# Linear attention on one core: the outputs of paired heads stored head by head

## The chip, the cores and the metric

The kernel runs on 1 core of one Trainium2 chip. The metric is the device time of one execution in microseconds. Before the change it is 180.78 us, the median of 3 runs (179.79 to 180.81).

A core has five engines that run their own instruction streams: PE (TensorE, matmuls), DVE (VectorE), ACT (ScalarE), POOL (GpSimd) and SP (SyncE, here used to issue DMA transfers). They are ordered against each other by semaphores only. Data move between the chip's main memory (DRAM in the names below) and the on-chip SBUF, which has 128 partitions, by 16 DMA engines. A transfer names two lists of addresses, one for each side, as nested steps and counts.

## The reference, cut to what matters

```python
B, H, S, D = 1, 32, 2048, 128        # q, k, v: [B, H, S, D] bf16

def reference(q, k, v):
    phi_q = jnp.where(q > 0, q + 1, jnp.exp(q)) + 1e-6
    phi_k = jnp.where(k > 0, k + 1, jnp.exp(k)) + 1e-6
    kv = jnp.einsum("bhsd,bhse->bhde", phi_k, v)
    z = jnp.einsum("bhsd->bhd", phi_k)
    num = jnp.einsum("bhqd,bhde->bhqe", phi_q, kv)
    den = jnp.einsum("bhqd,bhd->bhq", phi_q, z)[..., None] + 1e-6
    return num / den
```

Each of the 32 heads has 2048 rows of 128 numbers in q, k, v and in the output, 512 KB each.

## The kernel before

**Work per head.** k and v of a head are loaded whole (512 KB, 128 partitions of 16 rows, 4 KB each). phi is made in two parts that are added in PSUM by matmuls: `em` = min(exp(x), 1) + EPS and `rk` = max(x, 0). The matmuls `kv{h}` (L430) build the 128 x 129 matrix of kv and z, `kvs{h}` (L397) copies it to SBUF. q is transposed on PE (`T`, L445) to PSUM, from which ACT and DVE make its two parts (L465 and L386, L392). The matmuls `n{h}.{i}` (L495 to L502) give numerators and denominators, `r` (L522) takes reciprocals and `f{h}.{i}` (L526, DVE) writes the quotients to the output buffer `o_sb[:, h % NO]`, with NO = 14 buffers of one head each. A store `st` then takes them to DRAM.

**Paired heads.** Heads 4 to 27 (`pair(h)`, L23) are handled in twos for q. One 1 MB load brings q of two heads as 128 partitions of 8 KB: 64 partitions for each head, 32 rows in each partition. After the transposes the columns of the two heads are sorted apart, in the order j, head, b, r. So in the output buffer of a paired head, partition 64 b + r holds rows 32 r + 16 b + j of that head, for j from 0 to 15. The first 64 partitions (b = 0) hold the even blocks of 16 rows (4 KB), the other 64 (b = 1) the odd blocks.

**The stores before.** Unpaired heads are stored from 128 partitions in one or more parts given by `st_parts` (L536). Head 2 goes in rows 0:51, 51:115 and 115:128 (`ROWS`), head 3 in two halves of its tiles, the first of them in rows 0:68 and 68:128 (`HALF`), head 31 in three parts of its tiles. A pair is stored by two transfers (L543), one for each half c of the partitions: 64 partitions, two heads, 4 KB. Each waits for every `f` of both heads.

**What sets the order.** The order of the instructions on each engine is written out by hand (`ORDER`, L108). SP issues all loads but one and all stores, one after another; an instruction that waits on SP holds up all that stand behind it. `add` registers an operation with what it depends on, `fill` and `used` add the waits for a buffer's earlier users, and `resolve` turns them into semaphore waits. After the last load (`ldq31.0`) SP has the stores st16, st24, st20, st23, st21, st18, st28, st19, st27, st22, st29, st26, st30 and the three of head 31. At the end SP waits for the semaphores of all output buffers (L562).

Of the kernel before, what the change touches and what calls it, by code (L numbers as in the profile page):

```python
# [14 lines left out]
NO, NE, NR, NV, NQ, NK = 14, 2, 2, 2, 4, 2  # L15
# [7 lines left out]
def pair(h):  # L23
    return QFIRST <= h < QLAST
# [36 lines left out]
def groups(h):  # L61
    if h == NH - 1:
        return ((0, 2, 3, 0), (6, 2, 3, 2), (12, 2, 2, 4))
    return ((0, 4, 3, 0), (12, 2, 2, 4))
# [6 lines left out]
def st_parts(h):  # L71
    tiles = ((0, 6), (6, 12), (12, 16)) if h == NH - 1 else WHOLE
    if h in HALF:
        tiles = HALVES
    return tuple((a, b, x, y) for i, (a, b) in enumerate(tiles)
                 for x, y in (HALF.get(h, ()) if i == 0 and h in HALF else ROWS.get(h, ((0, P),))))
# [5 lines left out]
def eps_dve(h, i):  # L82
    return i == 1 or h in EPD


def on(key, eng):
    return ON.get(key, eng)
# [90 lines left out]
def _ap(base: bass.AP, elem_offset: int, dims):  # L178
    return bass.AP(base.tensor, base.offset + elem_offset, [list(base.ap[0])] + [list(d) for d in dims])


class Program:
# [10 lines left out]
    def add(self, eng, key, fn, deps=(), dma=None, inc=True):  # L193
        assert key not in self.op, key
        self.op[key] = (eng, fn, tuple(deps), dma, inc)
# [71 lines left out]
def bass_standalone__linear_attn_elu__prompt_kernel(nc: bass.Bass, q: bass.AP, k: bass.AP, v: bass.AP, out: bass.AP):  # L267
    B, H, S, D = q.shape
    assert D == P and S == 16 * P and B * H == NH
    NT = S // P  # L270
# [5 lines left out]
    qf, kf, vf, of = (t.rearrange("b h s d -> (b h) s d") for t in (q, k, v, out))  # L276
    rows = lambda t, h: t[h].rearrange("(p j) d -> p j d", j=NT)

    with ExitStack() as es:
# [17 lines left out]
        o_sb = sb([P, NO, NT, D])  # L297
# [8 lines left out]
        add = pr.add  # L306
# [3 lines left out]
        def over(name, h, parts, t0, t1):  # L310
            return [f"{name}{h}.{i}" for i, (a, b) in enumerate(parts(h)) if a < t1 and t0 < b]

        def every(name, h, parts):
            return [f"{name}{h}.{i}" for i in range(len(parts(h)))]

        def fill(buf, n, heads, key):
            slots = [(buf, h % n) for h in heads]
            for s, h in zip(slots, heads):
                if users.get(s, (None, None, None))[0] != h:
                    users[s] = (h, users[s][2] if s in users else [], [])  # L320
            return [d for s in slots for d in users[s][1]]

        def used(buf, n, heads, key):
            for h in heads:
                u = users[buf, h % n]
                assert u[0] == h, (buf, h, u[0])
                u[2].append(key)

        def fs(h, banks):
            return [f"f{h}.{i}" for i, (t0, nb, n, b0) in enumerate(groups(h))  # L330
                    if set(banks) & set(range(b0, b0 + nb))]

        def both(h, p=pair):
            return (h - h % 2, h - h % 2 + 1) if p(h) else (h,)

        def first(h):
            return both(h)[0]

        def rqs(h, t0=0, t1=NT):
            return [d for x in both(h) for d in  # L340
                    ([f"rqa{x}"] if t0 < na(x) else []) + over("rqb", x, rqb_parts, t0, t1)]
# [57 lines left out]
        def head(h):  # L399
# [75 lines left out]
            if blk == len(two) - 1:  # L475
                for x in two:
                    out_of(x)

        def out_of(h):
            two, h0 = both(h), first(h)  # L480
            blk = h - h0

            def tile(buf, t):
                if len(two) == 1:
                    return buf[:, h % NQ, t]
                return buf[:, h0 % NQ:h0 % NQ + 2].rearrange("p h j d -> p (h j d)")[:, (2 * t + blk) * P:(2 * t + blk + 1) * P]

            for i, (t0, nb, m, b0) in enumerate(groups(h)):
                late = eps_dve(h, i)

                def g(e, t0=t0, nb=nb, m=m, b0=b0, late=late):
                    for b in range(nb):
                        o = 512 * (b0 + b)
                        if not late:
                            e.matmul(_ap(o_ps[:, :], o + D, [[NC, m]]), lhsT=ones[:], rhs=epsr[:, 0:m], start=True,  # L495
                                     stop=False, skip_group_check=True)
                        for c in range(m):
                            t = t0 + b * m + c
                            to = o_ps[:, o + NC * c:o + NC * (c + 1)]
                            e.matmul(to, lhsT=tile(emq_sb, t), rhs=kvs_sb[:, h % NK, 0:NC], start=late and c == 0,  # L500
                                     stop=False, skip_group_check=True)
                            ins = e.matmul(to, lhsT=tile(rq_sb, t), rhs=kvs_sb[:, h % NK, 0:NC], start=False, stop=True,  # L502
                                           skip_group_check=True)
                    return ins
                banks = range(b0, b0 + nb)
                t1 = t0 + nb * m
                key = f"n{h}.{i}"
                add("PE", key, g, [d for x in two for d in over("emq", x, q_parts, t0, t1)] + [f"kvs{h}", "ones", "eps1", "eps2"] + rqs(h, t0, t1)
                    + (fs(h - 1, banks) if h else []) + ([f"kvs{h + 1}"] if 5 in banks and h + 1 < NH else []))
                for buf, n in (("emq", NQ), ("rq", NQ)):  # L510
                    used(buf, n, two, key)
                used("kvs", NK, (h,), key)
                den = _ap(o_ps[:, :], 512 * b0 + D, [[512, nb], [NC, m]])
                rden = rden_sb[:, h % 2, t0:t1].rearrange("p (a b) -> p a b", b=m)
                done = [key]
                if 5 in banks and h + 2 < NH and GAP == 3:
                    done += every("kv", h + 2, kv_parts) if on(f"kvs{h + 2}", "DVE") == "DVE" else [f"kvs{h + 2}"]
                if late:
                    add("DVE", f"a{h}.{i}", lambda e, rden=rden, den=den: e.tensor_scalar(  # L519
                        rden, den, EPS, None, op0=ALU.add), done)  # L520
                    done, den = [f"a{h}.{i}"], rden
                add("DVE", f"r{h}.{i}", lambda e, rden=rden, den=den: e.reciprocal(rden, den), done)  # L522

                def g(e, t0=t0, t1=t1, nb=nb, m=m, b0=b0):
                    first = lambda t: t.offset
                    return e.tensor_tensor(  # L526
                        out=_ap(o_sb[:, :, :, :], first(o_sb[:, h % NO, t0, 0:1]) - first(o_sb[:, :, :, :]),
                                [[m * D, nb], [D, m], [1, D]]),
                        in0=_ap(o_ps[:, :], 512 * b0, [[512, nb], [NC, m], [1, D]]),
                        in1=_ap(rden_sb[:, :, :], first(rden_sb[:, h % 2, t0:t0 + 1]) - first(rden_sb[:, :, :]),  # L530
                                [[m, nb], [1, m], [0, D]]), op=ALU.mult)
                add("DVE", f"f{h}.{i}", g, [f"r{h}.{i}"] + fill("o", NO, (h,), f"f{h}.{i}"))
            if len(two) == 1:
                for i, (a, b, x, y) in enumerate(st_parts(h)):
                    key = f"st{h}.{i}"
                    add("SP", key, lambda e, a=a, b=b, x=x, y=y: e.dma_start(rows(of, h)[x:y, a:b], o_sb[x:y, h % NO, a:b]),  # L536
                        [f"f{h}.{j}" for j, (t0, nb, m, b0) in enumerate(groups(h)) if t0 < b and a < t0 + nb * m],
                        dma=f"o{h % NO}")
                    used("o", NO, (h,), key)
            elif blk:  # L540
                for c in range(2):
                    key = f"st{h0 + c}.0"
                    add("SP", key, lambda e, c=c: e.dma_start(  # L543
                        of[h0:h0 + 2].rearrange("h (r b j) d -> b r h (j d)", b=2, j=NT)[c],
                        o_sb[64 * c:64 * c + 64, h0 % NO:h0 % NO + 2].rearrange("p h j d -> p h (j d)")),
                        [d for x in two for d in every("f", x, groups)], dma=f"o{(h0 + c) % NO}")
                    used("o", NO, two, key)

        for h in range(NH):
            head(h)  # L550
# [40 lines left out]
```

## Time and profile before

| | |
|---|---|
| median of 3 runs | 180.78 us |
| the profiled execution's own time | 180.66 us |
| its span, first to last instruction | 179.4 us |
| PE busy | 155.6 us (87%) |
| DVE busy | 157.2 us (88%) |
| ACT busy | 146.8 us (82%) |
| POOL busy | 82.4 us (46%) |
| DRAM read / written | 50.33 MB / 16.78 MB |
| SP's issue of a paired store (L543), min/median/max | 0.60 / 1.85 / 2.67 us |
| paired store, issue to landing, min/median/max | 8.0 / 13.7 / 17.6 us |
| SP's waits for buffers and results at loads (L382 and L243) | 45 us |
| SP's waits for DVE at paired stores | 7.1 us |

How to read the profile: the page gives busy times by engine, then the span in 40 equal slices in which a digit is the busy share in tenths, then the DMA queues with their packets. A packet is one contiguous run of bytes moved by one DMA engine. The DMA row is the mean busy share of the 16 engines, and GB/s is what they moved together. "Windows" are the same sums for chosen stretches: start and end in us, length, then busy time and number of instructions of PE, PE's weight loads, DVE, ACT and POOL, then the granted PE clock, the DMA share and GB/s. Lines such as L543 are lines of the kernel.

### The profile page before, as it was taken

To read this page: it belongs to the slowest core of one execution; us is meant where nothing else is said; L and a number is where in the kernel's file an instruction comes from. 1 tells how busy PE (TensorE), PEld (TensorE's weight loads), DVE (VectorE), ACT (ScalarE), POOL (GpSimd) and SP (SyncE) were. 2 spreads that over 40 slices of the span, in tenths; PEclk is the share of its full clock that TensorE was granted. 3 is DMA by queue.
4 is the path that set the end of the run, shared out by engine and by line. 5 is a ranking of instruction groups with operands and counts; after the bars stand their busy time and mean duration, and the time that the engine had idled before them with its cause. 6 is when DMAs were issued, how large, how long until landed. Compare 5 with 4: busy or idle time off the path is not lost.

```text
span 179.4 us, 6127 instructions
## 1 busy us (share of the span) xinstructions
PE 155.6 (87%) x2709; PEld 150.2 (84%) x2709; DVE 157.2 (88%) x309; ACT 146.8 (82%) x99; POOL 82.4 (46%) x62
## 2 busy tenths in 40 slices
PE   6589997899999999999999999999995999994000
PEld 2279987899999999999999999999995999994000
DVE  0499999999999999999999999999989999999200
ACT  3879979799999999999999999999879897880000
POOL 1000512866675666666656666666566468100000
PEclk9999999999999999999999999999999999999755
DMA  6999999999999999999999999999999999999995
GB/s 234 408 422 410 412 408 420 407 407 420 405 418 400 420 407 407 371 388 410 418 422 417 408 407 396 387 409 417 417 409 419 395 336 338 253 249 262 253 249 215
DMA packets 17182, 67.51 MB, mean 376 GB/s; under 512 B 1923, under 2 KB 2307, under 8 KB 15619
## 3 DMA queue, kind: packets, MB, share of 16 engines
q1 hardware_dynamic: 17011, 66.59, 97.3%
q8 instruction: 21, 0.34, 0.8%
q10 hardware_dynamic: 144, 0.52, 0.7%
q14 instruction: 6, 0.05, 0.1%
HBM read 50.33 MB, written 16.78 MB: 374 GB/s over the span
## 4 chain that ended last, share of the span: by engine, by line
PE 58%; DVE 18%; DMA 13%; ACT 1%; SPq 1%; issue 0%; ACTq 0%
PE la L430 23%; PE la L500 12%; PE la L445 12%; PE la L502 11%; DMA la<-in_k_dram 9%; DVE la L526 6%; DVE la L386 5%; DVE la L392 5%; DMA la<-in_v_dram 4%; SPq L543 1%; DVE la L422 1%; ACT la L410 1%; DVE la L522 1%; DVE la L397 1%; ACT L355 0%
## 5 line engine op out<-in xcount | busy, mean ns | idle before, releaser
L526 DVE TENSOR_TENSOR la<-la 128x1536 bf16<-128x1536 f32 (+1 forms) x65 | 77.9, 1199 | 0.7
L393 POOL TENSOR_SCALAR la<-la 128x2048 bf16<-128x2048 bf16 x27 | 52.0, 1925 | 42.0 <-PE la L430 40.9
L465 ACT ACTIVATE la<-la 128x2048 bf16<-128x2048 bf16 (+2 forms) x35 | 60.2, 1730 | 8.5 <-PE la L445 5.6
L500 PE MATMUL la<-la 128*128 128x129 bf16 x512 | 66.6, 219 | 0.0
L502 PE MATMUL la<-la 128*128 128x129 bf16 x512 | 66.6, 219 | 0.0
L430 PE MATMUL la<-la 128*128 128x129 bf16 x1024 | 63.4, 220 | 2.7 <-DVE la L422 2.6
L410 ACT ACTIVATE la<-la 128x2048 bf16<-128x2048 bf16 (+1 forms) x33 | 61.4, 1865 | 4.8 <-DMA la<-in_k_dram 4.1
L430 PEld LDWEIGHTS la<-la 128*128 128x128 bf16 x1024 | 59.3, 98 | 3.6 <-DVE la L422 3.0
L502 PEld LDWEIGHTS la<-la 128*128 128x128 bf16 x512 | 49.6, 97 | 0.0
L500 PEld LDWEIGHTS la<-la 128*128 128x128 bf16 x512 | 47.9, 97 | 0.3 <-DVE la L526 0.2
L386 DVE TENSOR_SCALAR la<-la 128x2048 bf16<-128x2048 bf16 (+2 forms) x68 | 44.1, 684 | 1.2 <-ACT la L410 1.2
L422 POOL COPY la<-la 128x1024 int32<-128x1024 int32 x29 | 30.8, 1062 | 28.2 <-PE la L430 21.2
L445 PE MATMUL la<-la 128*128 128x128 bf16 x512 | 34.2, 220 | 3.7 <-DVE la L392 3.4
L445 PEld LDWEIGHTS la<-la 128*128 128x128 bf16 x512 | 30.0, 98 | 5.5 <-DVE la L392 4.2
L391 ACT ACTIVATE la<-la 128x1024 bf16<-128x1024 bf16 (+3 forms) x29 | 31.9, 1099 | 0.0
L392 DVE TENSOR_SCALAR la<-la 128x1024 bf16<-128x1024 bf16 (+3 forms) x37 | 24.9, 677 | 4.2 <-DMA la<-in_k_dram 4.2
L495 PE MATMUL la<-la 128*128 128x3 bf16 (+1 forms) x128 | 21.5, 168 | 1.6 <-DVE la L526 1.6
L495 PEld LDWEIGHTS la<-la 128*128 128x128 bf16 x128 | 12.5, 98 | 1.8 <-DVE la L526 1.8
L522 DVE RECIPROCAL la<-la 128x12 f32<-128x12 f32 (+1 forms) x65 | 12.9, 199 | 1.3 <-PE la L502 0.5
L397 DVE CAST la<-la 128x129 bf16<-128x129 f32 x32 | 8.1, 255 | 0.0
L362 PE MATMUL la<-la 128*128 128x480 bf16 x21 | 6.1, 433 | 1.5 <-POOL la L347 1.5
L519 DVE TENSOR_SCALAR la<-la 128x4 f32<-128x4 f32 (+1 forms) x32 | 5.0, 157 | 0.3 <-PE la L430 0.2
(15 smaller groups left out, 7.2 us busy)
## 6 DMA issues: line engine op xcount, KB each, us to landing
la<-in_k_dram SPq DMA_DIRECT2D x32, 512.0 KB, 13.1
la<-in_v_dram SPq DMA_DIRECT2D x31, 512.0 KB, 13.8
out_dram<-la SPq DMA_DIRECT2D x29, 512.0 KB, 13.0
la<-in_q_dram SPq DMA_DIRECT2D x12, 1024.0 KB, 14.1
la<-in_q_dram SPq DMA_DIRECT2D x8, 512.0 KB, 12.0
la<-in_v_dram ACTq DMA_DIRECT2D x1, 512.0 KB, 6.6
out_dram<-la SPq DMA_DIRECT2D x2, 256.0 KB
out_dram<-la SPq DMA_DIRECT2D x2, 192.0 KB
```

What stands on the lines that cost most here:

```text
L386: add(on(key, "DVE"), key, lambda e: e.tensor_scalar(t, t, 1.0, EPS, op0=ALU.min, op1=ALU.add), deps)
L392: "DVE": lambda e: e.tensor_scalar(dst, src, 0.0, None, op0=ALU.max),
L393: "POOL": lambda e: e.tensor_scalar(dst, src, BIG, 0.0, op0=ALU.min, op1=ALU.max)}[eng], deps)
L410: add("ACT", key, lambda e, a=a, b=b: e.activation(em_sb[:, h % NE, a:b], k_sb[:, h % NI["k"], a:b], ACT.Exp), [f"ldk{k0}.0"] + fill("em", ...
L422: add(on(key, "POOL"), key, lambda e, a=a, b=b, word=word: e.tensor_copy(v1_sb[:, h % NV, a:b, 0:D].bitcast(word), v_sb[:, h % NI["v"], a: ...
L430: ins = e.matmul(kv_ps, lhsT=src[:, j], rhs=v1_sb[:, h % NV, j, 0:NC], start=(j + part == 0), stop=(j == NT - 1 and part == 1))
L445: ins = e.transpose(xT[:, j], src, ident[:])
L465: add("ACT", key, lambda e, a=a, b=b: e.activation(part(emq_sb, a, b), src(a, b), ACT.Exp), over("T", h, t_parts, a, b) + fill("emq", NQ, ...
L495: e.matmul(_ap(o_ps[:, :], o + D, [[NC, m]]), lhsT=ones[:], rhs=epsr[:, 0:m], start=True, stop=False, skip_group_check=True)
L500: e.matmul(to, lhsT=tile(emq_sb, t), rhs=kvs_sb[:, h % NK, 0:NC], start=late and c == 0, stop=False, skip_group_check=True)
L502: ins = e.matmul(to, lhsT=tile(rq_sb, t), rhs=kvs_sb[:, h % NK, 0:NC], start=False, stop=True, skip_group_check=True)
L526: return e.tensor_tensor(out=_ap(o_sb[:, :, :, :], first(o_sb[:, h % NO, t0, 0:1]) - first(o_sb[:, :, :, :]), [[m * D, nb], [D, m], [1, D] ...
```

## The change

The two transfers per pair, each half of the partitions of both heads, become two transfers each of all 128 partitions of one head. In DRAM the destination is listed as b (2 blocks, step 4 KB), r (64, step 8 KB) and 4 KB in one piece. The store of a head depends on that head's `f` alone, and an output buffer has one store as its user instead of two. The keys and their places in `ORDER` stay.

```diff
-            if len(two) == 1:
-                for i, (a, b, x, y) in enumerate(st_parts(h)):
-                    key = f"st{h}.{i}"
-                    add("SP", key, lambda e, a=a, b=b, x=x, y=y: e.dma_start(rows(of, h)[x:y, a:b], o_sb[x:y, h % NO, a:b]),
-                        [f"f{h}.{j}" for j, (t0, nb, m, b0) in enumerate(groups(h)) if t0 < b and a < t0 + nb * m],
-                        dma=f"o{h % NO}")
-                    used("o", NO, (h,), key)
-            elif blk:
-                for c in range(2):
-                    key = f"st{h0 + c}.0"
-                    add("SP", key, lambda e, c=c: e.dma_start(
-                        of[h0:h0 + 2].rearrange("h (r b j) d -> b r h (j d)", b=2, j=NT)[c],
-                        o_sb[64 * c:64 * c + 64, h0 % NO:h0 % NO + 2].rearrange("p h j d -> p h (j d)")),
-                        [d for x in two for d in every("f", x, groups)], dma=f"o{(h0 + c) % NO}")
-                    used("o", NO, two, key)
+            for i, (a, b, x, y) in enumerate(st_parts(h)):
+                key = f"st{h}.{i}"
+                to = rows(of, h)[x:y, a:b]
+                if pair(h):
+                    to = of[h].rearrange("(r b j) d -> b r (j d)", b=2, j=NT)
+                add("SP", key, lambda e, a=a, b=b, x=x, y=y, to=to: e.dma_start(to, o_sb[x:y, h % NO, a:b]),
+                    [f"f{h}.{j}" for j, (t0, nb, m, b0) in enumerate(groups(h)) if t0 < b and a < t0 + nb * m],
+                    dma=f"o{h % NO}")
+                used("o", NO, (h,), key)
```

## The prediction

> **What bounds the kernel now.** I read the page's chain of waits first. It gives PE 58% and the DMA only 13%, but a chain follows one thread of work. A queue that is always full hides behind it. So the page's second and third parts came next: the DMA rows of the 40 slices, the packet count and the row of queue 1, which carries everything that SP issues.
>
> ```profile
> span 179.4 us, 6127 instructions
> ...
> DMA  6999999999999999999999999999999999999995
> GB/s 234 408 422 410 412 408 420 407 407 420 405 418 400 420 407 407 371 388 410 418 422 417 408 407 396 387 409 417 417 409 419 395 336 338 253 249 262 253 249 215
> DMA packets 17182, 67.51 MB, mean 376 GB/s; under 512 B 1923, under 2 KB 2307, under 8 KB 15619
> ...
> q1 hardware_dynamic: 17011, 66.59, 97.3%
> ```
>
> The 16 DMA engines are busy from the first slice to the last: queue 1 alone fills 97.3% of their span. They move about 410 GB/s while loads run and about 250 GB/s in the last six slices. Then I read the windows, to get the rate of one engine in each stage (the last three columns are granted PE clock, DMA share and GB/s):
>
> ```profile
> 60.00:100.00 40.00, 40.00 (x732) 40.00 (x730) 39.69 (x81) 39.32 (x27) 25.82 (x18) 1.00 1.02 407
> ...
> 120.00:140.00 20.00, 17.78 (x322) 17.46 (x320) 19.07 (x36) 17.22 (x13) 11.62 (x8) 1.00 1.02 415
> ...
> 152.00:168.00 16.00, 11.49 (x204) 11.03 (x201) 14.17 (x29) 7.43 (x7) 1.26 (x1) 1.00 0.96 250
> ```
>
> With loads and stores mixed, sixteen full engines move 407 to 415 GB/s. I take 410, so 25.6 GB/s each. When only stores are left (152 to 168 us) they are just as busy (0.96) and move 250, so 15.6 GB/s each. From issue to landing a 512 KB transfer takes 13 us (part 6 of the page), ten times the 1.3 us that 410 GB/s would need: each engine has a backlog. The kernel ends when its fullest DMA engine has done its share. So the question for any change of a transfer is how its bytes are dealt over the 16 engines. Last I read the sizes of the stores:
>
> ```profile
> out_dram<-la SPq DMA_DIRECT2D x29, 512.0 KB, 13.0
> ...
> out_dram<-la SPq DMA_DIRECT2D x1, 204.0 KB
> out_dram<-la SPq DMA_DIRECT2D x1, 136.0 KB
> out_dram<-la SPq DMA_DIRECT2D x1, 128.0 KB
> out_dram<-la SPq DMA_DIRECT2D x1, 120.0 KB
> out_dram<-la SPq DMA_DIRECT2D x1, 52.0 KB
> ```
>
> Four of these tell how a transfer is dealt out. They are the rows of `ROWS` and `HALF`: 51 partitions (204 KB), 68 (136 KB), 60 (120 KB) and 13 (52 KB). The 128.0 KB row is head 31's last store, 128 partitions of 1 KB.
>
> **How a transfer is dealt over the engines, from the packet counts.** The data packets of queue 1 can be counted from the code, one for each contiguous row: k 32 x 128, v 31 x 128 (one v load goes by ACT), q 20 x 128, paired stores 24 x 64 x 2, the other stores 5 x 128 whole heads, 3 x 128 for head 31, 128 for head 2 and 68 + 60 + 128 for head 3. That is 15104. The page has 17011, so 1907 packets are something else; with the 16 of the one load on queue 10 they are the 1923 "under 512 B". Queue 1 carries 121 transfers, and 121 x 16 = 1936: one small completion packet for each engine that takes part, with 29 missing. If a transfer runs on the largest number up to 16 that divides its outermost count, the four odd stores run on 3, 4, 15 and 13 engines instead of 16, and 13 + 12 + 1 + 3 = 29 are missing. That is exact. So the outermost dimension is cut into equal whole steps and nothing finer is tried: 51 rows went to three engines although sixteen could have had three or four each. The 24 paired stores of before are 64 partitions by 2 heads by 4 KB on both sides, so they have their 16 engines; with any other number the sum would not close.
>
> **What the change does, part by part.**
> 1. *The new destination.* On the SBUF side the store becomes 128 partitions of 4 KB. On the DRAM side it is `b r (j d)`: outermost 2 (even or odd block, step 4 KB), then 64 (step 8 KB), then 4 KB. This list can't be merged, because the second half of the partitions starts 4 KB after the first, not after its end. Its outermost count is 2, and 2 can be cut into at most 2 equal whole steps. So I expect each of the 24 stores to run on 2 engines, 64 packets of 4 KB on each, instead of 8 packets on each of 16. In every transfer of before the two sides have the same outermost count, so the trace does not show which side decides when they differ; I take the one that can't be cut further. If the 2 are always the same engines, all other DMA waits for these two; rival F is the other case. [...]
> 2. *The load of these two engines.* All data are 66.59 + 0.52 = 67.11 MB. The 24 stores are 24 x 524288 B = 12.58 MB. The other 54.53 MB come to 3.41 MB on each engine, and about 0.08 MB more on the first ones from the odd stores (204/3 + 136/4 KB instead of 340/16): 3.5 MB. To this come 24 x 262144 B = 6.29 MB of new stores. At 25.6 GB/s: 3.5 MB take 137 us and 6.29 MB take 246 us, in sum 383 us. The price from both sides: 26.4 GB/s (422 GB/s, the fastest slices) gives 9.79 MB / 26.4 = 371 us, 15.6 GB/s for the new stores gives 137 + 403 = 540 us. I take 25.6, since 15.6 is measured with 16 engines writing at once, 250 GB/s in sum, and two engines at 25.6 write 51 GB/s in sum; from 100 to 140 us eight stores ran among the loads at 400 to 415 GB/s.
> 3. *What lies around it.* The DMA share of the first 4 us is about half, 1.8 us idle; the run takes 180.66 us against its span of 179.4, 1.3 us outside; after the last data comes under 1 us. So 383 + 4 = 387 us.
> 4. *Nothing hides it.* PE, DVE and ACT have at most 157 us of work each. In SP's order 10 paired stores, with heads 28 to 31 between them, come after the last load: 10 x 10.2 us on the two engines, during which the last heads' compute (now from the issue of the last load at 144 us to the last f at 167, 23 us) ends long before.
> 5. *Waits and queue order.* The stores keep their places in SP's order, their number and their 512 KB. Each now waits for its own head's f only, not for both heads. The wait of an f for its o buffer, 14 heads later, drops from two stores to one. SP's waits for DVE at these stores are 7.1 us in all (one of 6.8, one of 0.3), so that is the most they can return, and only where no backlog stands behind them: at full backlog nothing. What is new on SP is blocking: each store puts 64 packets on two engines that hold some 80 (13 us / 0.16 us a packet), so SP stands about 64 x 0.16 = 10 us at each, with the loads of later heads queued behind it. The other 14 engines then run dry, and k and v arrive at the pace of the two. This adds nothing of its own, since the sum already has all packets of the two engines; it costs only if they run dry too. SP's other waits (loads for free buffers, some 45 us in all now) bound that from above; with stores of 10 us between the loads most of them will have been met before SP gets there, so I take 0.
>
> **The rivals.**
> - *A, the forecast:* two engines at 25.6 GB/s, 387 us.
> - *B, stores slow down when they are alone.* The last 10 paired stores have no loads between them. If an engine then writes at the 15.6 GB/s of 152 to 168 us, they take 10 x 262144 B / 15.6 = 168 us instead of 102: 453 us. For it: the engines' busy share stays 0.96 there. Against it: that looks like a limit of all 16 writing at once.
> - *C, all new stores at 15.6 GB/s:* 540 + 4 = 544 us. Against it: the mixed stretch from 100 to 140 us.
> - *D, all 16 engines after all* (the other side): if the SBUF side alone decides, 128 partitions go over 16 engines as in the whole-head stores, with the same bytes and packets. Then the bytes still set the end, and the change can only return part of SP's 7.1 us of waits; the DMA share from 140 us on is 0.96 and lower, so idle DMA time is about 5% of 39 us, 2 us: 176 to 181 us. It decides if the completion packets of the 24 stores stay at 16 each.
> - *E, the two engines run dry* where loads wait for buffers behind a blocked SP: up to 45 us on A, 390 to 432 us.
> - *F, the pair of engines moves on from store to store.* Then eight pairs take three stores each, every engine has its 4.19 MB as before, and the price is the lumps: the last store lands up to 10 us late on its pair, and one before it may share that pair: 181 plus 10 to 20, 190 to 200 us. The trace of before can't exclude it.
>
> **How the numbers follow.** A 0.65, B 0.14, C 0.05, D 0.08, E 0.05, F 0.03. The predicted time is A's, 387 us. The range reaches from 366 us (1% under the 371 us of the fastest slices, since the share of one engine is only known as a mean of sixteen) to 470 us, B with a few us of E on top; it leaves out C, D and F, 0.16 in all. About 1% is what a measurement of this kernel can tell from no change. Faster by over 1% is half of D, 0.04; the same is the other half, 0.04; slower is all else, 0.92.
>
> **What would show it.** In the profile after: queue 1 with 24 x 14 = 336 packets fewer (16675), and 1587 packets under 512 B; a DMA share that falls to a few tenths once the paired stores begin at about 60 us, and to about 2/16 in the last 100 us; GB/s there near 51; SP issues of about 10 us at the paired stores; PE, DVE and ACT with the same busy time and long idle stretches put down to loads. If the packet counts are unchanged, step 1 is wrong and D holds. If the counts are as said and the last stretch shows 31 GB/s, B or C holds; if the DMA stays full with the counts lower, F does; if the share falls below 2/16 with loads still to come, E does.

## The result and the profile after

The changed kernel takes 377.2 us (median of 4 runs, 376.95 to 377.43). The kernel before took 180.3 us beside it. The ratio is 2.092, with a 95% interval of 2.084 to 2.100. The forecast was 387 us, in a range of 366 to 470. On the chips of the experiments below the kernel before took 177.3 to 182.6 us, and the ratios compare fast runs with fast runs (178 to 179 us of it on average), so they differ a little from the ratios of the medians.

The page of the changed kernel, the same rows as before: span, DMA share and GB/s in 40 slices (now 9.4 us each), packets, queue 1.

```profile
span 375.8 us, 6134 instructions
...
DMA  8999999855389418127146145112111112111321
GB/s 324 417 410 411 412 415 409 332 233 196 130 289 396 163 56 297 52 102 249 53 142 260 52 157 194 52 55 101 53 55 53 53 52 96 58 53 52 151 101 48
DMA packets 16846, 67.51 MB, mean 180 GB/s; under 512 B 1587, under 2 KB 1971, under 8 KB 15283
...
q1 hardware_dynamic: 16675, 66.59, 45.9%
```

The bytes are the same, 67.51 MB. The packets are 336 fewer, all of them small ones: 1587 instead of 1923. That is 24 x 14, so each of the 24 stores has lost 14 of its 16 completion packets. From the second to the sixth slice, before the paired stores, the DMA runs at 410 to 417 GB/s, as before. Then the rate falls to 52 or 53 GB/s wherever nothing but paired stores is under way, and the busy share to about an eighth. The windows of the last part say it without rounding to tenths (last columns: DMA share, GB/s):

```profile
280.00:300.00 20.00, 3.75 (x36) 3.49 (x36) 5.79 (x11) 0.00 (x0) 0.00 (x0) 0.54 0.13 53
300.00:320.00 20.00, 0.00 (x0) 0.00 (x0) 0.00 (x0) 0.00 (x0) 0.00 (x0) 0.50 0.19 76
320.00:340.00 20.00, 0.00 (x0) 0.00 (x0) 0.00 (x0) 0.00 (x0) 0.00 (x0) 0.50 0.13 52
```

A share of 0.13 is two engines of sixteen, and 52 or 53 GB/s are 26 on each. No two stores run on different pairs at once, or the share would be 4/16. The line with 0.19 holds one of the unpaired stores, which still spread over all engines.

SP's own timeline shows what this does to the queue (start, duration, what was issued):

```profile
121.14 9.54 SPq L538 DMA_DIRECT2D out_dram<-la  x2
130.73 9.74 SPq L382 DMA_DIRECT2D la<-in_v_dram  x1
...
246.97 9.73 SPq L382 DMA_DIRECT2D la<-in_q_dram  x1
256.75 107.19 SPq L538 DMA_DIRECT2D out_dram<-la  x16
```

Each store costs SP some 10 us, or the load right behind it does: a v load that took about 1 us to issue now stands for 9.7 us, about the time that one store's packets take on each of the two engines (by estimate 64 x 159 ns, the median of a 4 KB packet, or 10.2 us). And the waits of the other engines (us in total, times, longest):

```profile
ACT la L410 <- DMA la<-in_k_dram: 68.1, 7, 15.7
DVE la L526 <- DMA out_dram<-la: 67.0, 9, 15.3
POOL la L422 <- DMA la<-in_v_dram: 56.7, 6, 16.3
PEld la L445 <- DMA la<-in_q_dram: 48.2, 5, 14.7
```

PE, DVE and ACT are busy for 176, 163 and 148 us (156, 157 and 147 before) and wait for loads, and DVE's `f` for an output buffer whose store has not landed.

### The profile page after: what moved, and what is told of

Read it like the earlier page. It is cut to its first block, busy times and chain, and to the rows that moved or that the text cites. A ratio compares the mean times of both kernels' runs of the same rounds, so it can differ in the third digit from the quotient of the medians.

```text
span 375.8 us, 6134 instructions
## 1 busy us (share of the span) xinstructions
PE 176.3 (47%) x2709; PEld 168.2 (45%) x2709; DVE 162.9 (43%) x309; ACT 147.5 (39%) x99; POOL 83.7 (22%) x62
## 2 busy tenths in 40 slices
DMA packets 16846, 67.51 MB, mean 180 GB/s; under 512 B 1587, under 2 KB 1971, under 8 KB 15283
## 3 DMA queue, kind: packets, MB, share of 16 engines
q1 hardware_dynamic: 16675, 66.59, 45.9%
## 4 chain that ended last, share of the span: by engine, by line
DMA 30%; SPq 19%; PE 12%; DVE 8%; ACT 3%; issue 3%; POOL 2%; POOLq 0%; ACTq 0%; DVEq 0%
DMA la<-in_k_dram 11%; SPq L382 10%; SPq L538 9%; DMA la<-in_v_dram 8%; DMA out_dram<-la 6%; DMA la<-in_q_dram 5%; PE la L430 4%; PE la L445 3%; PE la L500 2%; DVE la L526 2%; PE la L502 2%; DVE la L392 2%; DVE la L386 2%; ACT la L410 2%; POOL la L422 1%
## 5 line engine op out<-in xcount | busy, mean ns | idle before, releaser
L502 PE MATMUL la<-la 128*128 128x129 bf16 x512 | 75.1, 235 | 0.0
L500 PE MATMUL la<-la 128*128 128x129 bf16 x512 | 74.8, 232 | 0.5 <-DVE la L397 0.3
L393 POOL TENSOR_SCALAR la<-la 128x2048 bf16<-128x2048 bf16 x27 | 52.8, 1958 | 79.9 <-DMA la<-in_k_dram 43.6
L445 PE MATMUL la<-la 128*128 128x128 bf16 x512 | 39.8, 239 | 62.6 <-DMA la<-in_q_dram 46.6
L430 PE MATMUL la<-la 128*128 128x129 bf16 x1024 | 68.3, 229 | 1.6 <-DVE la L422 1.5
L430 PEld LDWEIGHTS la<-la 128*128 128x128 bf16 x1024 | 64.5, 103 | 2.6 <-DVE la L422 1.9
L445 PEld LDWEIGHTS la<-la 128*128 128x128 bf16 x512 | 34.7, 108 | 65.7 <-DMA la<-in_q_dram 48.2
L386 DVE TENSOR_SCALAR la<-la 128x2048 bf16<-128x2048 bf16 (+2 forms) x68 | 48.4, 744 | 35.7 <-ACT la L410 21.8
L502 PEld LDWEIGHTS la<-la 128*128 128x128 bf16 x512 | 53.1, 104 | 0.0
L500 PEld LDWEIGHTS la<-la 128*128 128x128 bf16 x512 | 51.9, 105 | 1.2 <-DVE la L526 0.7
L495 PEld LDWEIGHTS la<-la 128*128 128x128 bf16 x128 | 13.2, 103 | 45.4 <-DVE la L526 31.4
```

Source lines behind the costliest of these rows:

```text
L386: add(on(key, "DVE"), key, lambda e: e.tensor_scalar(t, t, 1.0, EPS, op0=ALU.min, op1=ALU.add), deps)
L393: "POOL": lambda e: e.tensor_scalar(dst, src, BIG, 0.0, op0=ALU.min, op1=ALU.max)}[eng], deps)
L430: ins = e.matmul(kv_ps, lhsT=src[:, j], rhs=v1_sb[:, h % NV, j, 0:NC], start=(j + part == 0), stop=(j == NT - 1 and part == 1))
L445: ins = e.transpose(xT[:, j], src, ident[:])
```

## The experiments

All start from the changed kernel unless said otherwise. The times are medians; the ratio is to the kernel before on the same chip.

| run | paired heads are stored as | us | ratio (95%) |
|---|---|---|---|
| the change | 128 partitions, DRAM list 2 x 64 | 377.2 | 2.092 (2.084 to 2.100) |
| e3 | 128 partitions, 4 x 32 | 258.0 | 1.447 (1.430 to 1.464) |
| e4 | 128 partitions, 8 x 16 | 204.7 | 1.148 (1.131 to 1.165) |
| e1 | 2 x 64 partitions | 171.8 | 0.965 (0.956 to 0.974) |
| e2 | 128 partitions, 128 rows | 168.4 | 0.945 (0.939 to 0.952) |
| e6 | 2 x 64 partitions, 64 rows without step | 172.7 | 0.964 (0.952 to 0.976) |
| e7 | as before, without step | 181.7 | 1.018 (1.007 to 1.028) |
| e9 | as e1, waits for both heads | 172.0 | 0.958 (0.942 to 0.975) |
| e10 | as before, halves adjacent | 176.0 | 0.984 (0.968 to 1.000) |
| e8 | no pairs, 128 partitions, 128 rows | 169.1 | 0.947 (0.935 to 0.959) |

### e1: the same addresses and waits in two transfers of 64 partitions

```diff
+    if pair(h):
+        return ((0, 16, 0, 64), (0, 16, 64, 128))
...
-                    to = of[h].rearrange("(r b j) d -> b r (j d)", b=2, j=NT)
+                    to = of[h].rearrange("(r b j) d -> b r (j d)", b=2, j=NT)[x // 64]
```

The first lines stand in `st_parts`. In `ORDER` each `st{h}.0` of a paired head is followed by its `st{h}.1`.

> Per-head stores as in the changed kernel, with the same waits and the same addresses in DRAM (step of 8 KB), but each in two transfers of 64 partitions, whose outermost count is 64 on both sides. Theory (the outermost count of 2 on the DRAM side puts each store on two engines): 16 engines again, 1923 + 24 x 16 = 2307 packets under 512 B, DMA share near 1 until the end, 178 to 183 us. Rival 1 (the 8 KB step or the even and odd 4 KB blocks make DRAM writes slow): stays near 377 us. Rival 2 (a head's store alone, or its one-head wait, upsets the order of the queue): stays well above 190 us.

171.8 us. The page's rows:

```profile
span 169.6 us, 6158 instructions
...
DMA packets 17566, 67.51 MB, mean 398 GB/s; under 512 B 2307, under 2 KB 2691, under 8 KB 16003
```

2307 small packets, as the theory says: 16 for each of the 48 transfers. The addresses in DRAM and the waits are those of the change, so neither the 8 KB step nor the one-head store is what doubled the time. What was not expected is that it is 3.5% faster than before; e6 to e10 follow that up.

### e2: the same transfer to a list that merges

```diff
-                if pair(h):
-                    to = of[h].rearrange("(r b j) d -> b r (j d)", b=2, j=NT)
```

> The store of a paired head stays one transfer of 128 partitions with the wait for its own head, but its destination is the 128 contiguous rows of 4 KB that an unpaired head has (the rows of paired heads then lie in another order in the output: the interleaving of even and odd blocks is left out). Theory: outermost count 128 on both sides, 16 engines, 1923 packets under 512 B, 176 to 183 us. Rival 2 (one-head stores and waits): above 190 us. It also prices what 128 partitions a store are worth beside 64: if 64 partitions were what slowed the stores at the end to 250 GB/s, this is 5 us or more faster than before; I expect less than 2 us.

168.4 us with 1923 small packets. The transfer has the same 128 partitions on the SBUF side as in the change. Only the DRAM list differs, 128 x 4 KB instead of 2 x 64 x 4 KB. So where the sides differ, as in the change, the outermost count of 2 on the DRAM side was enough to confine the transfer (1587 small packets, 14 fewer for each store). My other figure was wrong: I expected less than 2 us against before, and by the ratio it is about 10. The same window of before and of e2, when few or no loads are left (last column GB/s):

```profile
152.00:164.00 12.00, 10.39 (x187) 10.12 (x185) 11.30 (x23) 7.43 (x7) 1.26 (x1) 1.00 0.96 256
```

```profile
152.00:164.00 12.00, 8.44 (x149) 7.90 (x146) 11.14 (x25) 4.82 (x5) 0.00 (x0) 1.00 0.99 399
```

Before moves 256 GB/s there, e2 399, both with full engines (shares of 0.96 and 0.99). So stores alone do not limit the DMA to 250 GB/s.

### e3 and e4: four and eight engines

The edit of e3; e4 has b=8.
```diff
-                    to = of[h].rearrange("(r b j) d -> b r (j d)", b=2, j=NT)
+                    to = of[h].rearrange("(r b j) d -> b r (j d)", b=4, j=NT)
```

> As the changed kernel, but the destination is listed as 4 x 32 x 4 KB instead of 2 x 64 x 4 KB (rows of paired heads lie in another order in the output). Theory: four engines for each paired store, 32 packets on each; 1923 - 24 x 12 = 1635 packets under 512 B; the fullest engines have 3.5 + 24 x 0.131 = 6.64 MB, at the 26.2 GB/s of the changed kernel 254 us, with 3 us around it 257 us. Rival 1 (the interleaved list is slow in itself, whatever its outermost count): near 377 us.

> As the changed kernel, but the destination is listed as 8 x 16 x 4 KB (rows of paired heads lie in another order in the output). Theory: eight engines for each paired store, 16 packets on each; 1923 - 24 x 8 = 1731 packets under 512 B; the fullest engines have 3.5 + 24 x 0.0655 = 5.07 MB, 193 us at 26.2 GB/s, with 3 us around it 196 us, up to 210 us if eight engines writing at once already get in each other's way. Rival 1: near 377 us.

258.0 us against 257 expected, and 204.7 against 196 (up to 210). The page of e3:

```profile
GB/s 279 419 413 407 422 403 417 407 413 414 414 399 342 185 317 402 384 181 327 192 170 332 125 263 318 111 346 171 105 169 105 105 108 104 167 105 167 175 158 91
DMA packets 16894, 67.51 MB, mean 263 GB/s; under 512 B 1635, under 2 KB 2019, under 8 KB 15331
```

and of e4:

```profile
DMA packets 16990, 67.51 MB, mean 333 GB/s; under 512 B 1731, under 2 KB 2115, under 8 KB 15427
```

The small packets are 1635 and 1731, exactly the counts for 4 and 8 engines. Where e3 has only paired stores under way it moves 105 GB/s, four times 26. The time follows the bytes of the fullest engine as the prediction counts them (0.08 MB from the odd stores included, an estimate that no run shows): 9.79 MB 377 us, 6.64 MB 258 us, 5.07 MB 205 us. The first two steps agree within 1% with 26.2 GB/s and 3 us around it. The third is 9 us over. Part of that lies at its end:

```profile
184.00:200.00 16.00, 0.00 (x0) 0.00 (x0) 0.00 (x0) 0.00 (x0) 0.00 (x0) 0.50 0.63 199
```

A share of 0.63 is 10 engines at work, and 199 GB/s are 20 on each instead of 26. That is a quarter of these 16 us, so by estimate 4 of the 9. Why eight engines on stores run slower here, and where the rest goes, is open.

### e6 and e7: 64 partitions or the 8 KB step?

e1 and e2 differ in both. e6 is e1 and e7 is the kernel before, each storing to rows without a step:

```diff
-                    to = of[h].rearrange("(r b j) d -> b r (j d)", b=2, j=NT)[x // 64]
+                    to = of[h].rearrange("(b r j) d -> b r (j d)", b=2, j=NT)[x // 64]
...
-                        of[h0:h0 + 2].rearrange("h (r b j) d -> b r h (j d)", b=2, j=NT)[c],
+                        of[h0:h0 + 2].rearrange("h (b r j) d -> b r h (j d)", b=2, j=NT)[c],
```

> Two transfers of 64 partitions per paired head, as in e1, but to contiguous rows of 4 KB (rows of paired heads lie in another order in the output). e1 took 171.8 us and e2 168.4 us; they differ in two things: 64 partitions a transfer instead of 128, and the 8 KB step in DRAM. Theory P (a transfer of 64 partitions slows the engines when stores follow stores, whatever its addresses in DRAM): as e1, 170.5 to 173 us, some hundreds of 4 KB packets of twice 159 ns near the end. Rival S (the 8 KB step does it): as e2, 167.5 to 169.5 us.

> The kernel before, with its two transfers per pair (64 partitions, two heads) and its waits for both heads, but to contiguous rows of 4 KB inside each head (rows of paired heads lie in another order in the output). Theory P (64 partitions a transfer): as before, 179 to 182 us, with about 250 GB/s once stores are alone. Rival S (the 8 KB step): 168 to 173 us and 380 GB/s or more there.

172.7 and 181.7 us: neither is faster than its counterpart with the step. e6 has the ratio of e1 (0.964 and 0.965), and e7 is 1.8% slower than before. So leaving out the step gains nothing, and what is left between e1 and e2 is the 64 partitions of a transfer. The number of transfers is not it: before and e2 have 24 each for the paired heads. The trace has the time of each packet. A 4 KB packet takes 159 ns at the median in all these runs, but with stores of 64 partitions a part of them takes twice that (packets of queue 1):

| run | 4 KB packets over 250 ns, of 12928 | their median |
|---|---|---|
| before | 926 | 312 ns |
| e7 | 854 | 312 ns |
| e10 | 508 | 312 ns |
| e6 | 299 | 318 ns |
| e1 | 214 | 322 ns |
| e9 | 178 | 318 ns |
| e2 | 68 | 373 ns |

In before four fifths of them lie in the last 30 us, where a third to a half of the packets are slow. Earlier, among loads, at most 7% of the packets in any 10 us are. The changed kernel, e3 and e4 are another case: 334 to 381 of their packets take over 250 ns, with medians of 354 to 381 ns, and what slows those is open. That 312 ns are about twice 159 goes with the 256 GB/s of before against the 399 of e2; why a part of the packets takes twice the time there is not shown by a run.

### e9 and e10: why e1 beats before with the same 64 partitions

e9 gives e1's transfers the waits of before; e10 is the kernel before with the two transfers of a pair side by side in SP's order (the lines after the "...", in `orders`).

```diff
+                    [d for z in (two if pair(h) else ()) for d in every("f", z, groups)] +
                     [f"f{h}.{j}" for j, (t0, nb, m, b0) in enumerate(groups(h)) if t0 < b and a < t0 + nb * m],
...
+    for h in range(QFIRST, QLAST, 2):
+        at = min(keys["SP"].index(f"st{h}.0"), keys["SP"].index(f"st{h + 1}.0"))
+        keys["SP"] = [x for x in keys["SP"] if x not in (f"st{h}.0", f"st{h + 1}.0")]
+        keys["SP"][at:at] = [f"st{h}.0", f"st{h + 1}.0"]
```

> As e1 (two transfers of 64 partitions per paired head, the two halves one behind the other), but each transfer waits for the f of both heads of its pair, as the kernel before does. It tells apart what made e1 9 us faster than before. Theory H (first and second half alternate in the queue, so the engines read from all 128 partitions more of the time): as e1, 170.5 to 173.5 us. Rival W (the wait for one head only): near 180 us.

> The kernel before, with the two transfers of each pair one behind the other in SP's order, at the place of the earlier one, so that first and second half of the partitions alternate, in steps of 512 KB instead of e1's 256 KB. Theory H: faster than before, 172 to 177 us, with fewer slow packets near the end. Rival W: 179 us or more, since the waits for both heads stay and stores come no later in the queue.

By its ratio e1 is 6 us faster than before, not 9. e9 takes 172.0 us, as e1. So the wait for one head instead of two, which is all that the change brings besides its address lists, is worth nothing measurable here. e10 takes 176.0 us, though its interval ends at 1.000, and its edit also brings the later store of a pair forward; its slow packets say more than its time. The finer the two halves of the partitions alternate in the queue, the fewer slow packets: 926 in before, 508 in steps of 512 KB, 178 to 299 in steps of 256 KB, 68 in e2, where each transfer has all 128 partitions on 16 engines.

### e8: a version that beats both

```diff
 def pair(h):
-    return QFIRST <= h < QLAST
+    return False
```

In `ORDER` each `ldq` of a pair is followed by the load of the pair's second head.

> As the changed kernel, but q of all heads is loaded head by head (12 loads of 1 MB become 24 of 512 KB, the second of a pair right behind the first in SP's order), so that no head's rows are interleaved and every head is stored by one transfer of 128 partitions to contiguous rows, waiting for itself alone. Theory P: stores of 128 partitions on 16 engines, so near e2: 168.4 us plus 12 x 8 packets of 8 KB at 309 ns that become 2 of 159 ns, 0.9 us on each engine, 169.3 us, and 400 GB/s or so until the last 5 us. Rival: 24 instead of 12 loads on SP, or the wait for one more load, upset the order: 173 us or more. If P's number holds, this is the version that beats both kernels with the reference's output.

```profile
span 167.8 us, 6159 instructions
...
GB/s 204 401 419 412 406 407 410 403 406 409 417 405 411 410 406 409 412 421 412 411 415 414 415 412 404 417 413 414 418 414 422 413 418 413 414 417 391 412 407 258
```

169.1 us against 169.3 expected, 5.3% faster than before. All slices but the first and last run at 391 to 422 GB/s. The pairs bought packets of 8 KB for q (309 ns instead of two of 159) and paid for them with stores that fit only half of the partitions or, in the change, only two engines.

## Why the prediction was right

- **Step 1, two engines instead of 16: right.** The counts came out as written, 16675 packets and 1587 small ones. e2, e3 and e4 tie them to the outermost count of the DRAM list: 128, 4 and 8 give 16, 4 and 8 engines with the same SBUF side. That it is always the same pair, which the trace of before could not show, is seen in the share of 0.13; F is out. By that share, and by the 377 us, the same two carry all; which two, no view here names.
- **Step 2, the load of the two: right, 2% mis-sized.** 9.79 MB were to take 383 us at 25.6 GB/s. The tail shows 26 GB/s on each, and 9.79 MB at 26.2 are 374 us. The 25.6 was a mean of sixteen engines over slices of mixed work. These 9 us are nearly the whole gap between 387 and 377; the rest is step 3, 3 us around the sum instead of 4. That the two engines also carry the 0.08 MB of the odd stores, 3 us of the sum, was my estimate and is shown by no run. The runs showed 26 GB/s on each in the tail and 377.2 us in all; without the 0.08 MB, 26.2 GB/s and 3 us around the sum give 374 us.
- **Stores alone at 15.6 GB/s (B and C): out, but in part by luck.** I called that figure "a limit of all 16 writing at once" and took 25.6 for two engines because of it. e2 has all 16 writing at 399 GB/s, so there is no such limit at 250; the slow tail of before (256 GB/s) comes with its stores of 64 partitions. The choice between A at 387 and B and C at 453 and 544 us was right, for a reason that does not hold. The other reason, eight stores from 100 to 140 us, holds for stores among loads only. Why the changed kernel's last stores run at 26 GB/s an engine, and not at 15.6, was not tested.
- **D, 16 engines after all: did not occur, and was priced wrong.** I gave it 176 to 181 us, by the idle share of the engines. e2 is D's transfer but for the step in DRAM, which e6 and e7 show to be worth nothing, and takes 168.4. A busy share of 0.96 hid that up to half of the tail's packets took 312 ns at the median instead of 159. Had the destination been one that merges, D's price would have missed a gain of 5%.
- **Step 5, waits and queue order: half right.** SP stands about 10 us at a store, or at the load behind it. E, two engines run dry, is out: in the trace's packet records queue 1 has at least two packets under way at every moment from 60 to 300 us, and later on all but 0.6 us. That most of SP's waits at loads would have been met was wrong: they are 50 us (45 before). They cost nothing, because the two engines had work all the while. And the step left out that `f`, with one store to wait for instead of two, would wait 67 us for its buffer; that wait too ran beside the work of the two engines.
- **Step 4, the compute ends long before: right.** The last `f` begins at 288 us of 376.

## What to carry to other kernels

Look at the outermost count of both address lists of a transfer. In these runs a DRAM list that starts with 2 put half a megabyte on two engines (a DMA share of 0.13, 52 GB/s), although the SBUF side had 128 partitions, and everything queued behind it waited (SP some 10 us a store). Written as two transfers with an outermost count of 64 (e1), or as one with 128 (e2), it had all 16 (2307 and 1923 small packets). In these runs the number of small completion packets on the page told how many engines the transfers used: 1923 with 16 for each paired store, 1731 with 8, 1635 with 4, 1587 with 2. It can be read before any change is made. A DMA share near 1 did not say that the DMA was at its rate (0.96 at 256 GB/s, 0.99 at 399): compare GB/s between stages, and where stages of equal share differ, look at how many partitions their transfers touch (64 and 128 here) and at the times of single packets (312 ns and 159).

## What the runs showed that was not expected

Stores of 64 partitions in the order of before ran at 256 GB/s (152 to 164 us), stores of 128 at 399. With the two halves of the partitions in turn, as in e1, those of 64 ran at 341 (152 to 168 us). Mixed with loads the 64 were hidden (409 GB/s in e7 from 100 to 140 us). In the starved kernel the granted PE clock fell to between 0.54 and 0.80 in the 20 us windows from 100 to 300 us, and the large matmuls took 229 to 239 ns on average instead of 220. The compute still ended at 289 us, long before the last store.
